# The last two blocks of a first MoE layer as one stage: its first product by seven block products on 512-column halves, with the second block's activations kept in DRAM

## The chip, the cores and the metric

The kernel runs on one core of a Trainium2 chip. The metric is the device time of one execution in microseconds. Every engine follows its own instruction list in order: TensorE (PE) multiplies, VectorE (DVE) and ScalarE (ACT) do the elementwise work, and SyncE (SP) issues nearly all DMAs. They wait for one another by semaphores.

## The reference

Chunked attention over 4 x 768 tokens (8 heads of 64) gives x of 3072 x 512. Two feed-forward layers follow:

```python
x = attention(q, k, v, mem_k, mem_v)          # 3072 x 512
h = x @ w_in                                  # first layer: 512 -> 2048
g = np.maximum(h, 0.0) + alpha * np.minimum(h, 0.0)
x = g @ w_out                                 # 2048 -> 512
h = x @ w2_in                                 # second layer
out = (h * np.tanh(softplus(h))) @ w2_out
```

## The kernel before

**Tiles.** The tokens are six blocks of 512 columns (`NBA`, `BN`); x of a block is held transposed, four tiles of 128 rows. The 2048 inner features are 16 tiles j (`NJ`). Each fp32 operand is held as two fp32r parts, high and low, and a product is three matmuls: high by high, high by low, low by high. A "split" is a ScalarE cast for the high part and a VectorE subtraction for the low part.

**First layer.** For each block and j, `gemm1` (L990) does 4 x 3 matmuls of 512 columns into a bank, `act1` (L1019) applies the two-sided ReLU (two ScalarE steps, one VectorE step at L1025) and splits the result (L1015, L1016), and `gemm2` (L1059) does 4 x 3 matmuls of 512 columns into the block's four accumulating banks, two tiles j later (`LAG`). `evac` (L1065) sends a finished block's sums to `yd` in DRAM.

**Weights.** The first layer's are loaded and split once, in block 0. w1_in stays in 16 slots `wi`. Of w1_out, j from 10 on (`AWAY`) are also stored to `w1o` in DRAM (L1377), and in later blocks `reload1` (L396) brings them back through three slots in turn, 512 KB each.

**Second layer's weights.** 16 jobs of `spill` (L343; `w2_jobs`) load, convert and combine the weights for a scheme of seven block products in place of eight, and store the results in DRAM. They are spread over blocks 1 to 4. In block 5 `reload_in` (L408) brings what stays resident back into the `wi` and `wo` slots, 20 reloads of 512 KB.

**Attention.** Tiles of 128 tokens, T, go in pairs: a burst of score matmuls ("s", L723), softmax on ScalarE and VectorE with 16 VectorE transposes (L877), a burst of value matmuls ("v", L789), and a split into the block's x. The steps of block b + 1 are woven into the 32 half-steps of block b (`weave`, two per j). There is one set of buffers for scores and transposes; the keys and values of an odd tile share the tiles `upper` (L522, L559).

**Second layer.** For each of six blocks and eight pairs of j, `pair2` (L1160) does the seven products of 6 matmuls with 256 columns and the activation, and `gemm2_pair` the second product, 42 matmuls, woven between by `take`. `load_x` (L1087) prepares its operands from `yd`.

**Order.** `Plan` (L68) fixes the order of every engine's list ahead of time. Each step has a duration by formula (`a_`, `d_`, `p_`, `dma_`), a due time derived from the TensorE steps that need it, and dependences. Whenever an engine is free, the ready step with the earliest due time is next. A TensorE step that is not ready is passed by another that is. The chip then runs these lists as they stand.

Of the kernel before, what the change touches and what calls it, by code (L numbers as in the profile page):

```python
# [173 lines left out]
def chunked_attention_moe_moe_kernel(  # L174
# [77 lines left out]
    def dma_(b):  # L252
        return max(0.45, b / 265e3)
# [30 lines left out]
    AWAY = 10  # L284
    w1o = dp.tile([P, NJ - AWAY, 1024], F32, name="w1o")
# [110 lines left out]
    def reload1(u):  # L396
        w = slot("o", AWAY + away[0] % 3, [P, 2, 512], F32R)
        away[0] += 1
        add(
            "sp", dma_(P * 4096), lambda: nc.sync.dma_start(w.t.rearrange("p z f -> p (z f)").bitcast(F32), w1o[:, u - AWAY, :]),  # L400
            [(w1o_buf, u)], [w],
        )
        weights[0, "o", u] = w

    in_places = sorted([(j, "i", j) for j in range(12)] + [(j + 2, "o", j) for j in range(8)])
    pieces = {}

    def reload_in(n):  # L408
        w = slot(*in_places[n][1:], [P, 1024], F32R)
# [366 lines left out]
    def values_late(T):  # L776
# [19 lines left out]
        def rest():  # L796
            blk = T * P // BN
            if blk not in xts:
                xts[blk] = new_x(BN)
            (x, views, _, _), = xts[blk]  # L800
            cols = slice(T * P - blk * BN, (T + 2) * P - blk * BN)

            def unit(z, e):
                return views()[z][:, :, cols].rearrange("p a (i e n) -> p i a e n", i=2, e=2)[:, :, :, e]

            def flat(e):
                return bks[e].t.rearrange("p (i a n) -> p i a n", i=2, a=NP)

            def high(e):
                nc.scalar.copy(unit(0, e), flat(e))  # L810

            def low(e):
                nc.vector.tensor_sub(unit(1, e), flat(e), unit(0, e).bitcast(F32))

            for e in range(2):
                add("act", a_(512), partial(high, e), [bks[e]], [(x, ("h", T), e)])
                add("dve", d_(512), partial(low, e), [bks[e], (x, ("h", T), e)], [(x, ("l", T), e)])
# [66 lines left out]

    def behind(T):
# [42 lines left out]
    for blk in range(1, NBA):  # L928
        steps = []
        for T in range(blk * TB, (blk + 1) * TB, 2):  # L930
            steps += [("s", T), None, ("t", T) if T < UPT else None, ("v", T)]
        block_steps.append(steps)
# [5 lines left out]
    def open_second():  # L938
# [6 lines left out]

        def late(shape, tag):
            def make():
                open_()
                return phase["bp"].tile(shape, F32, tag=tag, name=tag)

            return make

# [12 lines left out]
        second["late"] = late  # L965
# [549 lines left out]
```

## Time and profile before

| | us |
|---|---|
| median of 3 runs | 1083.0 (1082.01 to 1083.23) |
| the profiled execution | 1082.07 |
| its span | 1080.3 |
| TensorE busy | 1073.4 (99%) |
| VectorE busy | 728.1 (67%) |
| ScalarE busy | 656.3 (61%) |
| DMA, mean over the span | 233 GB/s |

The first layer lies between about 25 and 590 us, with attention woven in until about 485 us; the second layer takes the rest. Busy shares are means over stages with different limits, so the reading goes by windows. The duration of a step can run into the next one's start; what an engine can carry is read from the distance of starts.

### The profile page before, as it was taken

How to read it: one execution, taken by the hardware profiler on the slowest of the kernel's cores; microseconds unless marked ns; L12 is line 12 of the kernel's file. 1: busy time of each engine (PE TensorE's matmuls, PEld its weight loads, DVE VectorE, ACT ScalarE, POOL GpSimd, SP SyncE). 2: the span in 40 equal slices, each digit the busy share in tenths (PEclk: the TensorE clock that was granted, in tenths of full speed). 3: DMA queues.
4: the chain of work that ended last, by engine and by line, in shares of the span. 5: the costliest groups of instructions: out<-in, count | busy, mean ns of one | idle time of the engine just before them, and what ended most of it. 6: DMA issues, size and time to landing. Idle time of an engine off the chain costs nothing.

```text
span 1080.3 us, 24504 instructions
## 1 busy us (share of the span) xinstructions
PE 1073.4 (99%) x9305; PEld 967.0 (90%) x9305; DVE 728.1 (67%) x1609; ACT 656.3 (61%) x1674; POOL 6.5 (1%) x19
## 2 busy tenths in 40 slices
PE   9999999999999999999999999999999999999998
PEld 6888888888888888888888999999999999999998
DVE  6899487676869767685422855675675675675654
ACT  6888456466564646555433766666676676675664
POOL 2000000000000000000000000000000000000000
PEclk9999999999999999999999999999999999999999
DMA  9968755776476577547764777887887887887874
GB/s 284 312 208 243 243 184 177 238 254 196 170 255 214 173 240 255 193 142 230 256 192 146 253 231 256 270 259 255 271 261 252 274 259 254 270 260 235 267 247 159
DMA packets 139670, 252.11 MB, mean 233 GB/s; under 512 B 13856, under 2 KB 45088, under 8 KB 139552
## 3 DMA queue, kind: packets, MB, share of 16 engines
q1 hardware_dynamic: 139552, 250.54, 72.3%
q8 instruction: 73, 1.20, 0.5%
q14 instruction: 45, 0.37, 0.1%
HBM read 205.14 MB, written 45.35 MB: 232 GB/s over the span
## 4 chain that ended last, share of the span: by engine, by line
PE 99%; ACT 0%; DVE 0%; issue 0%; DVEq 0%; ACTq 0%
PE bank L1003 24%; PE bank L1051 24%; PE bank L1267 22%; PE bank L1184 22%; PE bank L789 2%; PE bank L723 1%; PE bank L1361 1%; PE bank L600 0%; PE bank L667 0%; PE bank L836 0%; PE bank L860 0%; ACT L1198 0%; DVE e L1292 0%; ACT rstrip L250 0%; DVE rstrip L1326 0%
## 5 line engine op out<-in xcount | busy, mean ns | idle before, releaser
L1003 PE MATMUL bank<-xh,wi 128*128 128x512 f32 (+1 forms) x784 | 254.9, 387 | 0.0
L1051 PE MATMUL bank<-gh,wo 128*128 128x512 f32 x768 | 253.7, 391 | 0.0
L1003 PEld LDWEIGHTS bank<-xh,wi 128*128 128x128 f32 x784 | 146.3, 188 | 30.1
L1192 ACT COPY v<-bank 128x512 f32<-128x512 f32 x192 | 102.5, 534 | 115.0 <-PE bank L1184 112.0
L1051 PEld LDWEIGHTS bank<-gh,wo 128*128 128x128 f32 x768 | 144.1, 188 | 30.3
L1003 PE MATMUL bank<-xl,wi 128*128 128x512 f32 (+1 forms) x392 | 151.0, 385 | 0.0
L1051 PE MATMUL bank<-gl,wo 128*128 128x512 f32 x384 | 149.5, 389 | 0.0
L1025 DVE SCALAR_TENSOR_TENSOR rstrip<-rstrip,nalpha 128x512 f32<-128x512 f32 x96 | 71.8, 748 | 71.2 <-ACT rstrip L1022 70.4
L1015 ACT CAST gh<-rstrip 128x512 fp32r<-128x512 f32 x96 | 60.2, 627 | 89.0 <-DVE rstrip L1025 48.7
L1021 ACT ACTIVATE rstrip<-bank 128x512 f32<-128x512 f32 x96 | 57.9, 603 | 87.6 <-PE bank L1003 85.5
L1195 DVE TENSOR_TENSOR v<-v,v 128x256 f32<-128x256 f32 x190 | 79.5, 423 | 43.2 <-ACT v L1192 41.6
L1016 DVE TENSOR_TENSOR gl<-rstrip,gh 128x512 fp32r<-128x512 f32 x96 | 66.3, 691 | 56.0 <-ACT gh L1015 55.4
L1198 ACT ACTIVATE v<-v 128x256 f32<-128x256 f32 x192 | 80.0, 418 | 35.9 <-DVE v L1195 33.4
L1195 DVE TENSOR_TENSOR v<-v 128x256 f32<-128x256 f32 x142 | 60.0, 422 | 51.9 <-ACT v L1192 48.5
L1003 PEld LDWEIGHTS bank<-xl,wi 128*128 128x128 f32 x392 | 73.6, 188 | 14.4
L1051 PEld LDWEIGHTS bank<-gl,wo 128*128 128x128 f32 x384 | 72.1, 188 | 14.6
L1184 PE MATMUL bank<-wo,wi 128*128 128x256 f32 x432 | 61.9, 283 | 0.6 <-ACT v L1192 0.6
L742 ACT ACTIVATE s<-bank,su 128x64 f32<-128x64 f32 x160 | 48.5, 346 | 19.7 <-DVE su L759 19.7
L1022 ACT ACTIVATE rstrip<-bank 128x512 f32<-128x512 f32 x96 | 57.4, 598 | 0.9 <-DMA yd<-rstrip 0.9
L877 DVE STREAM_TRANSPOSE aT<-s 32x256 f32<-32x256 f32 x128 | 55.8, 436 | 2.9
L1184 PEld LDWEIGHTS bank<-wo,wi 128*128 128x128 f32 x432 | 56.3, 192 | 1.1 <-ACT v L1192 1.0
L1184 PE MATMUL bank<-xl,wi 128*128 128x256 f32 x396 | 54.4, 283 | 0.0
(198 smaller groups left out, 1888.0 us busy)
## 6 DMA issues: line engine op xcount, KB each, us to landing
wi<-w2o SPq DMA_DIRECT2D x201, 256.0 KB, 3.6
wo<-w2o SPq DMA_DIRECT2D x132, 256.0 KB, 3.7
wo<-w1o SPq DMA_DIRECT2D x30, 512.0 KB, 4.5
w2o<-wo SPq DMA_DIRECT2D x57, 256.0 KB, 2.6
wi<-w2s SPq DMA_DIRECT2D x56, 256.0 KB, 3.5
wo<-in_w_out_dram SPq DMA_DIRECT2D x24, 512.0 KB, 7.8
w2k<-wo SPq DMA_DIRECT2D x40, 256.0 KB, 2.2
wo<-w2s SPq DMA_DIRECT2D x40, 256.0 KB, 3.4
```

Of the source, the lines that this page charges most:

```text
L1003: nc.tensor.matmul(bk.t[:, lo:hi], a, b, start=kk == 0 and i == 0, stop=kk == KT - 1 and i == 2)
L1015: add("act", a_(n), lambda: nc.scalar.copy(g.t[0], src.t[0]), [src], [(g, "h")])
L1016: add("dve", d_(n), lambda: nc.vector.tensor_sub(g.t[1], src.t[0], g.t[0].bitcast(F32)), [src, (g, "h")], [(g, "l")])
L1021: add("act", a_(n) - 0.05, lambda: nc.scalar.activation(m.t[0], h.t[:, :n], AF.Relu, scale=-1.0), [h], [m])
L1022: add("act", a_(n) - 0.05, lambda: nc.scalar.activation(r.t[0], h.t[:, :n], AF.Relu), [h], [r])
L1025: lambda: nc.vector.scalar_tensor_tensor(r.t[0], m.t[0], nalpha[:, j : j + 1], r.t[0], ALU.mult, ALU.add),
L1051: nc.tensor.matmul(bk.t[:, :n], lt, rh, start=j == 0 and i == 0, stop=j == NJ - 1 and i == 2)
L1184: nc.tensor.matmul(X.t[:, half * HB : (half + 1) * HB], l, r, start=start and kk == n == 0, stop=kk == 1 and n == 2, skip_group_check=True,)
L1192: add("act", c_(n * HB), lambda: nc.scalar.copy(e.t[:, : n * HB], X.t[:, : n * HB]), [X], [(e, i) for i in range(n)])
L1195: add("dve", e_(HB), lambda: op(at(to), at(a), at(b)), [v[a], v[b]], [v[to]])
L1198: add("act", c_(HB), lambda: nc.scalar.activation(at(name), at(name), AF.Mish), [], [v[name]])
L1267: nc.tensor.matmul(bk.t[:, s * HB : (s + 1) * HB], g.t[:, zg * HB + s * P : zg * HB + (s + 1) * P], piece()[:, zw * HB : (zw + 1) * HB], s ...
```

## The change

Blocks 0 to 3 (`WIDE` = 4) are done as before. Their x, and that of blocks 4 and 5, is prepared earlier: the attention steps of blocks 2 to 5 are set at fixed half-steps of blocks 1 to 3 (`AT`: per pair scores at 0, values at 10, the next scores at 11). x of block 4 goes to four free `wo` slots (`far_x`). Eleven of the 16 `spill` jobs run in the first 38 tiles after block 0, and five in the new stage. `AWAY` becomes 6, and all 16 tiles of w1_out are stored to `w1o`, so every later use of j from 6 on, and of all j in the new stage, is a reload.

The new stage takes blocks 4 and 5 together. `wide_x` forms four combinations of the four 256 x 512 quarters of x (12 VectorE steps and 4 casts of 1024 columns). For each pair p of j, `sums_of_w` forms the four combinations of the weights' quarters and splits them; `pair1` does seven products of 6 matmuls with 512 columns, recombines them in banks and on VectorE, applies the activation to four 128 x 512 results, splits the two of block 4 for its `gemm2` and stores the two of block 5 to `rb` in DRAM. The parts of block 4's `gemm2` of the pair before are woven between (`take(12)`, two parts of three matmuls). After the pairs, block 5's activations are loaded from `rb`, split and multiplied, 14 tiles j after one another, with the weights reloaded a second time. `reload_in` runs partly in the stage, partly behind it and, for the last four, behind the end of block 5. The second layer's accumulators change banks (`ACC`, `X` from bank 7 to 3), its v tiles become halves of five tiles of 1024 columns, and `dma_` assumes 315 GB/s after 120 us of TensorE work.

The diff, cut:

```diff
-        return max(0.45, b / 265e3)
+        return max(0.45, b / (265e3 if plan.now < 120 else 315e3))
-    AWAY = 10
-    w1o = dp.tile([P, NJ - AWAY, 1024], F32, name="w1o")
+    AWAY = 6
+    WIDE = NBA - 2
+    JOBS, JOB_STEPS = 11, 38
+    w1o = dp.tile([P, NJ, 1024], F32, name="w1o")
+    rb = dp.tile([P, NJ, BN], F32, name="rb")
-    in_places = sorted([(j, "i", j) for j in range(12)] + [(j + 2, "o", j) for j in range(8)])
+    in_places = [("i", j) for j in range(2, 12)] + [("o", j) for j in range(6)] + [("i", 0), ("i", 1), ("o", 6), ("o", 7)]
...
+    block_steps.append(sum(([("s", T), None, ("t", T), ("v", T)] for T in range(TB, UPT, 2)), []))
+    AT = sum(((11 * n, 11 * n + 10) for n in range(8)), ())
+    steps_at = {2 * NJ + p: ("sv"[n % 2], UPT + n // 2 * 2) for n, p in enumerate(AT)}
...
-        second["X"] = bank(7)
+        second["X"] = bank(3)
-    ACC = {1: 4, 0: 5, 3: 6, 5: 0, 4: 1, 6: 2, 2: 3}
+    ACC = {1: 0, 0: 1, 5: 2, 3: 6, 4: 7, 6: 4, 2: 5}
...
+    def wide_x():
...
+        t = dict(zip(("a21", "a22", "a11", "a12"), second["whole"]))
+        for name in ("a21", "a22", "a11", "a12"):
...
+                "dve", d_(1024), lambda to=t[name], f=f: nc.vector.tensor_add(to.t, f(0).bitcast(F32), f(1).bitcast(F32)),
...
+        for name, to, a, b, op in (
+            ("s1", "a22", "a21", "a22", nc.vector.tensor_add), ("s3", "a21", "a11", "a21", nc.vector.tensor_sub),
+            ("s2", "a11", "a22", "a11", nc.vector.tensor_sub), ("s4", "a12", "a12", "a11", nc.vector.tensor_sub),
+        ):
...
+            add("act", a_(1024), lambda f=f, o=t[to]: nc.scalar.copy(f(0), o.t), [t[to]], [(bufs[0], "h")])
+            add(
+                "dve", d_(1024), lambda f=f, o=t[to]: nc.vector.tensor_sub(f(1), o.t, f(0).bitcast(F32)),
...
+    def sums_of_w(p):
+        w = [weights[0, "i", 2 * p + n] for n in range(2)]
+        tt, to = second["tt"].next(), wide["t"].next()
+        for n in range(2):
...
+        for to_, x, y in ((3, 5, 3), (5, 4, 5), (4, 4, 3), (6, 6, 4)):
+            add("dve", d_(HB), lambda to_=to_, x=x, y=y: nc.vector.tensor_sub(q(to_), q(x), q(y)), [], [tt])
+        add("act", a_(1024), lambda: nc.scalar.copy(to.t[:, :1024], tt.t), [tt], [(to, "h")])
...
+    def pair1(p, xs, take):
+        to = tops.pop(p)
+        A, B_ = (bank(i + p % 2 * 2) for i in (4, 5))
+        e1, e2, e3, e4 = (second["v"].next() for _ in range(4))
...
+            add("pe", 6 * 0.227, go, [w] + bufs, [bk])
...
+        product(0, A, True)
+        product(3, B_, True)
+        keep(e1, A)
+        keep(e2, B_)
+        take(12)
+        product(4, A, False)
+        product(2, B_, False)
+        keep(e3, A)
+        more(e3, B_)
+        act(j1, e3)
+        split_wide(WIDE, j1, e3)
+        take(12)
+        product(5, A, False)
+        more(e2, A)
+        act(j1, e2)
+        if not last_:
+            away_(j1, e2)
+        take(12)
+        product(6, A, False)
+        product(1, B_, True)
+        more(e1, B_)
+        act(j0, e1)
+        split_wide(WIDE, j0, e1)
+        act(j0, e4, A)
+        if not last_:
+            away_(j0, e4)
+        return e4, e2
...
+    open_second()
+    xs = wide_x()
+    open_wide()
+    for layer, blk, j in pend:
+        reload1(j)
+        parts.extend((6, part) for part in gemm2_parts(layer, blk, j))
+    tops = {0: sums_of_w(0)}
+    for p in range(NPAIR):
+        if p + 1 < NPAIR:
+            tops[p + 1] = sums_of_w(p + 1)
+        if p < 6:
+            for job in [next(jobs, None) for _ in range(1)]:
+                if job:
+                    job(plan.now + 25.0)
+        ends_ = pair1(p, xs, take)
+        take(12)
+        if 0 < p < 6:
+            for n in (2 * p - 2, 2 * p - 1):
+                reload_in(n)
+        if p < NPAIR - 1:
+            for j in (2 * p + 1, 2 * p):
+                parts.extend(wide_parts(WIDE, j, (p, j) == (0, 1), False))
...
+    for n, (e, j) in enumerate(zip(ends_[::-1], (NJ - 1, NJ - 2))):
+        for name, part in wide_parts(WIDE, j, False, j == NJ - 2):
+            part()
+        split_wide(WIDE + 1, j, e)
+        for name, part in wide_parts(WIDE + 1, j, n == 0, False, True):
+            part()
+    open_rest()
+    xnext = load_x(0)
+    for n in range(10, 16):
+        reload_in(n)
+    order_b = list(range(NJ - 2))
+    for j in order_b:
+        e = second["v"].next()
+        add("sp", dma_(P * BN * 4), lambda e=e, j=j: nc.sync.dma_start(e.t, rb[:, j, :]), [(rb_buf, j)], [e])
+        split_wide(WIDE + 1, j, e)
+        parts.extend(wide_parts(WIDE + 1, j, False, j == order_b[-1]))
+        while len(parts) > 8:
+            take(6)
...
+    for n in range(16, len(in_places)):
+        reload_in(n)
+    open_rings()
```

## Rows read from the trace of the kernel before

**Rows 1.** page: the span, and each engine's busy time, share and instructions

```profile
span 1080.3 us, 24504 instructions
...
PE 1073.4 (99%) x9305; PEld 967.0 (90%) x9305; DVE 728.1 (67%) x1609; ACT 656.3 (61%) x1674; POOL 6.5 (1%) x19
```

**Rows 2.** page: the chain that ended last, shares of the span

```profile
PE 99%; ACT 0%; DVE 0%; issue 0%; DVEq 0%; ACTq 0%
```

**Rows 3.** waits of TensorE: line, releaser, us in total, times, longest us

```profile
PE bank L1361 <- DVE busy L1359: 1.2, 1, 1.2
...
PE bank L1184 <- ACT v L1192: 0.6, 1, 0.6
```

**Rows 4.** chain in order of time, 35 to 170 us: start us, us, what

```profile
42.42 2.72 PE bank L1051 x12
...
152.76 2.00 PE bank L789 x128
154.76 2.95 PE bank L1003 x12
...
165.87 1.44 PE bank L723 x94
```

**Rows 5.** windows: us, busy per engine, PEclk, DMA share, GB/s

```profile
40.00:60.00 20.00, 20.00 (x94) 16.59 (x93) 18.83 (x39) 18.63 (x59) 0.00 (x0) 1.00 0.98 258
320.00:340.00 20.00, 20.00 (x90) 16.57 (x89) 18.97 (x43) 10.02 (x27) 0.00 (x0) 1.00 0.86 292
520.00:540.00 20.00, 20.00 (x90) 16.57 (x89) 5.06 (x8) 6.84 (x12) 0.00 (x0) 1.00 0.68 223
515.00:520.00 5.00, 5.00 (x23) 4.13 (x22) 4.80 (x8) 2.84 (x5) 0.00 (x0) 1.00 0.98 365
100.00:105.00 5.00, 5.00 (x142) 4.21 (x141) 4.97 (x10) 3.79 (x7) 0.00 (x0) 1.00 0.26 99
```

**Rows 6.** timeline of VectorE, three stretches: start us, us, line, operation

```profile
44.81 0.75 DVE L1025 SCALAR_TENSOR_TENSOR rstrip<-rstrip,nalpha 128x512 f32<-128x512 f32 x1
45.48 0.68 DVE L338 TENSOR_TENSOR wi<-wf,wi 128x512 fp32r<-128x512 f32 x1
46.08 0.42 DVE L323 TENSOR_SCALAR wf<-wo 128x512 uint32<-128x512 uint32 x1
46.54 0.69 DVE L326 SCALAR_TENSOR_TENSOR wf<-wo,wf 128x512 uint32<-128x512 uint32 x1
...
148.21 1.81 DVE L877 STREAM_TRANSPOSE aT<-s 32x256 f32<-32x256 f32 x4
...
324.71 0.42 DVE L364 TENSOR_TENSOR wo<-wf,wf 128x256 f32<-128x256 f32 x1
325.05 0.42 DVE L364 TENSOR_TENSOR wo<-wf 128x256 f32<-128x256 f32 x1
...
325.72 0.68 DVE L750 TENSOR_TENSOR s<-s,su 128x512 f32<-128x512 f32 x1
326.33 0.42 DVE L364 TENSOR_TENSOR wo<-wf,wo 128x256 f32<-128x256 f32 x1
```

**Rows 7.** groups by form, VectorE: count, busy us, mean ns, idle before

```profile
L1025 DVE SCALAR_TENSOR_TENSOR rstrip<-rstrip,nalpha 128x512 f32<-128x512 f32 x96 | 71.8, 748 | 71.2 <-ACT rstrip L1022 70.4
L1016 DVE TENSOR_TENSOR gl<-rstrip,gh 128x512 fp32r<-128x512 f32 x96 | 66.3, 691 | 56.0 <-ACT gh L1015 55.4
...
L1292 DVE TENSOR_TENSOR rstrip<-bank,rstrip 128x512 f32<-128x512 f32 x24 | 16.5, 688 | 3.8 <-PE bank L1267 3.0
...
L364 DVE TENSOR_TENSOR wo<-wf,wo 128x256 f32<-128x256 f32 x32 | 13.5, 421 | 0.3
```

**Rows 8.** line L400, the reloads of w1_out: issue to landing

```profile
DMA to landing us min/median/max: 3.7/4.5/6.8
```

**Rows 9.** line L522, an odd tile's keys: queue timeline from 154 us, and landing

```profile
154.47 1.21 SPq L522 DMA_DIRECT2D qbd<-in_kw_dram  x2
...
DMA to landing us min/median/max: 2.3/2.9/7.9
```

More of the change, by code (lines that the diff above doesn't have):

```diff
@@ L948, in make, with open_rest @@
                 open_()
-                return phase["bp"].tile(shape, F32, tag=tag, name=tag)
-            return make
+                if tag not in boxes:
+                    boxes[tag] = phase["bp"].tile(shape, F32, tag=tag, name=tag)
+                return boxes[tag]
+            return make
+        second["late"] = late
+        wholes = [late([P, 1024], f"b{i}") for i in range(5)]
+        second["whole"] = [Buf(m, att_bufs) for m in wholes]
+        second["tt"] = Ring(wholes[4:])
+        second["tt"].last = [att_bufs]
+        second["v"] = Ring([lambda m=m, i=i: m()[:, i * BN : (i + 1) * BN] for m in wholes[:4] for i in range(2)])
+        second["v"].last = [[b] for b in second["whole"][:4] for _ in range(2)]
+    def open_rest():
+        late = second["late"]
         def places(*tags):
@@ new lines, in chunked_attention_moe_moe_kernel, with open_wide @@
+    wide = {}
+    def open_wide():
+        makes = [lambda z=z: xmakers[1][z]() for z in range(2)]
+        wide["t"] = Ring(makes)
+        wide["t"].last = [list(xring.last[1]) for _ in range(2)]
+        gm = [lambda i=i: [t[:, i * BN : (i + 1) * BN] for t in gstrip.tiles] for i in range(2)]
+        for j in range(2):
+            m = maker(cp, [P, 2, 512], F32R, f"wi{j}")
+            gm.append(lambda m=m: (lambda w: [w[:, z, :] for z in range(2)])(m()))
+        g4.makes = gm
+        g4.last = [[x[2] for x in gstrip.live]] * 2 + [slots["i", 0], slots["i", 1]]
@@ new lines, in split_wide, with wide_parts, part, go @@
+    def split_wide(blk, j, e):
+        g = g4.next()
+        add("act", a_(BN), lambda: nc.scalar.copy(g.t[0], e.t), [e], [(g, "h")])
+        add("dve", d_(BN), lambda: nc.vector.tensor_sub(g.t[1], e.t, g.t[0].bitcast(F32)), [e, (g, "h")], [(g, "l")])
+        gts[0, blk, j] = g
+    def wide_parts(blk, j, first, last_, again=False):
+        if not again:
+            reload1(j)
+        w = weights[0, "o", j]
+        g = gts.pop((0, blk, j))
+        if first:
+            accs[0, blk] = [bank(a) for a in ((0, 1, 2, 3) if blk == WIDE else (6, 7, 4, 5))]
+        def part(a):
+            bk = accs[0, blk][a]
+            def go():
+                cs = slice(a * P, (a + 1) * P)
+                (gh, gl), (wh, wl) = g.t, (w.t[:, z, :] for z in range(2))
+                for i, (lt, rh) in enumerate(((wh[:, cs], gh), (wh[:, cs], gl), (wl[:, cs], gh))):
+                    nc.tensor.matmul(bk.t, lt, rh, start=first and i == 0, stop=last_ and i == 2)
+            add("pe", 3 * p_(BN), go, [w, g], [bk])
+            if last_:
+                evac(0, blk, a, bk)
+        return [(6, partial(part, a)) for a in range(KT)]
@@ L1389, in chunked_attention_moe_moe_kernel @@
     LAG = 2
[L1390 removed]
+    tiles = [(0, blk, j) for blk in range(WIDE) for j in range(NJ)]
     pend = []
     xcur = xts[0]
[L1393 to L1394 removed]
+    jobs = iter(w2_jobs)
+    sent_ = [0]
     for half in range(2):
```

175 lines of the change are left out of this document (125 added, 50 removed).

## The prediction

> **What bounds the kernel now.** I read first the busy times and the chain that ended last: TensorE is busy 1073.4 of 1080.3 us, and the chain is TensorE for 99% of the span [rows 1, 2]. Then the waits of TensorE, which name only 1.2 us and 0.6 us [rows 3]: nothing that the other engines or the DMAs do delays it after the start. Then the chain in order of time: a stretch of twelve 512-column matmuls (one `gemm1` or one `gemm2`) takes 2.72 us, so 0.2267 us each [rows 4]. Last, VectorE by windows: 18.8 and 19.0 of 20 us beside a full TensorE in the first layer, but 5.1 of 20 in its last block [rows 5]. So time is bought only by TensorE instructions, as long as VectorE and the DMAs still keep ahead; the change takes instructions from the first and gives work to the other two.
>
> **What is removed.** For two blocks and a pair of j, `gemm1` issues 2 x 2 x 12 = 48 matmuls of 512 columns; seven products of six matmuls are 42. Over 8 pairs 6 x 8 = 48 matmuls go: 48 x 0.2267 = 10.88 us. `gemm2`, the second layer and attention keep their matmuls. All of it lies on the path. The profiled execution took 1082.07 us (span 1080.3 and 1.8 around it), so with no new wait it becomes 1071.2. The median of the runs shown, 1083.0, lies 0.9 above that execution; I forecast on the execution and let the range take the 0.9.
>
> **Attention, packed.** Blocks 2 to 5 keep their 8 steps of each kind, but a score burst now starts one 2.72 us stretch after the value burst before it, where before it came 165.87 - 154.76 = 11.1 us after [rows 4]. The odd tile's keys go into `upper`, which the value burst reads, so they can only be loaded after it. Both loads were issued in 1.2 us, beginning at the burst's end, and one lands 2.9 us after its issue [rows 9]: about 0.9 + 2.9 = 3.8 us against 2.72. The planner charges these DMAs too (two of 0.55, 2.0 to land and 0.2: 3.3 us) and moves other matmuls ahead of the burst; what is left is what it misjudges, 0 to 0.6 us for each of 7 bursts: 0 to 4 us. I take 1.2, nearer to zero, because an order made by the same cost model leaves TensorE 0.6 us of waits after the start [rows 3]. Queued behind a late key load on SP are the next values and the stores of `spill`; nobody needs those within 10 us.
>
> **VectorE in blocks 1 to 3.** Its cost is read from starts, not durations: a 256-column tensor_tensor starts 0.34 us after the one before (its row says 0.42), a 512-column one 0.61 (0.68), the scalar_tensor_tensor 0.67 (0.75), a dependent pair 0.46 [rows 6]. From 256 and 512 a 1024-column one is estimated at 0.61 + 2 x 0.27 = 1.15. A pair of attention tiles now comes every 5.5 tiles, 5.5 x 5.44 + 3.95 (its bursts and their restarts) = 33.9 us. VectorE work in it: attention 16 transposes of 0.46 and six 512-column steps with small ones, 11.3; `act1` and splits 5.5 x 1.4 = 7.7; 5.5 x 11/38 = 1.6 `spill` jobs of 5.8 (two loads' conversions 2.1, eleven 256-column steps 3.7): 9.3. Together 28.3 of 33.9, 84%. Blocks 0 and 3 ran at 94 and 95% over 20 us with TensorE full [rows 5]: cost 0, since a tile's `act1` has about 10 us until its `gemm2`. Were that cover gone, each us over would be a us of TensorE.
>
> **Storing all of w1_out.** Ten more 512 KB stores fall around block 0, where the DMAs are at a quarter from 100 to 105 us [rows 5] and no store has a reader before block 1: cost 0. If they pushed a weight load back instead, one store is 1.4 us of them at 365 GB/s [rows 5]; 0 to 1.4, in the range only.
>
> **Entry into the wide stage.** Block 5's x is complete after the value burst of T=22, eight stretches (21.8 us) before the stage; `keep(e1)` and product 4 need the splits of s1, s3 and s2 some 4.1 us later (products 0 and 3 and two parts). In those 25.8 us VectorE must do two x splits 1.2, four adds, three sums and three splits of 1024 columns 10 x 1.15 = 11.5, the weight sums of pair 0 (two of 512, four of 256, one of 1024 and restarts) 4.1, and five tiles 6.4: 23.2, or 90%. It fits, with 2.6 us to spare. 0 to 3 us; I take 0.8, for the rise to 100% in places.
>
> **The wide pairs.** A pair is 42 + 24 matmuls = 14.96 us of TensorE. VectorE: three adds from PSUM 1.8, four scalar_tensor_tensor 2.7, two splits 1.2, weight sums 4.1: 9.8 us; with a `spill` job in pairs 0 to 4 it is 15.6, with none 9.8. Over eight pairs that is 8 x 9.8 + 5 x 5.8 = 107 of 120 us. Five pairs are 0.6 us over, 3.2 in all, unless the jobs, due 25 us later than issued, slide into pairs 5 to 7. In each pair product 6 waits for the add from the same bank, with 1.36 us of parts as cover for a 0.61 us step. Bounds 0 and 3.2; I take 1.3. ScalarE gets fourteen steps and a job's nine in 15 us; from 40 to 60 us it did 59 in 20 beside a full TensorE [rows 5]: 0.
>
> **The block that comes back from DRAM.** Fourteen j follow each other every 2.72 us, not 5.44, with three slots for the weights. A slot lives landing + 2.72 us of use, and three stretches last 8.16, so a load has 5.44 us. It lands in 4.5 us (median) and 6.8 (worst) [rows 8]. At 4.5 nothing is lost; at 6.8 a round takes 9.52, (9.52 - 8.16)/3 = 0.45 us per j, 6.3 us in all. Demand in the 49 us after the pairs: 16 weights 8.4 MB, 14 activations 3.7, x of the second layer 1.0, six reloads 3.1: 16.2 MB, 331 GB/s, against 365 GB/s in the fullest 5 us near there [rows 5]; the six reloads can begin in pair 7, where only two weights and two stores move, 1.6 MB in 15 us. Bounds 0 and 6.3; I take 1.0.
>
> **Start of the second layer.** Its first product gets bank 3, free earlier than bank 7 was, and four reloads move behind it, needed six pairs later. The 0.6 us wait there [rows 3] may go or stay: -0.6 to 0; I take 0.
>
> Sum: 1071.2 + 1.2 + 0.8 + 1.3 + 1.0 = 1075.5 us.
>
> **Rivals.** A, VectorE becomes the bound of the wide stage, and the kernel gets slower. If an instruction held the engine for its whole row, a pair would cost 3 x 0.688 + 4 x 0.748 + 2 x 0.691 for the splits + 2 x 0.691 + 4 x 0.421 + an estimated 1.23 for the sums = 10.7, and a job 2 x (0.42 + 0.69) + 11 x 0.421 = 6.9 [rows 6, 7]: 17.6 against 14.96, 2.6 us in each of five pairs, 13.1. With the attention and return terms, 1071.2 + 13.1 + 2.2 = 1086.5. It decides from 10.88/5 = 2.2 us over per pair. Against it: the starts overlap the rows before them [rows 6]. For it: the hand-over add, product 6, add couples the two engines in every pair. [...]
>
> B, the return from DRAM cannot keep its weights ahead of their use: 6.3 us at the worst landing in place of 1.0, 1075.5 + 5.3 = 1080.8. For it: reloads, activations and x share one queue in order, and a reload ahead adds its transfer. Against: all but the steady two loads can be done early.
>
> C, attention comes late. In the trace the last transposes of a pair end at 150.0, and the value burst stands at 152.8 [rows 4, 6]; the new order has one stretch (2.72 us) less from scores to values, so no slack is left unless VectorE, which works by due time, does them earlier. Late by 2.7 us at the last pair, and with key loads at their bound of 4, it is 1071.2 + 4 + 2.7 + 0.8 + 1.3 + 1.0 = 1081.0.
>
> D, the saving is not there: the matmuls removed do not set the pace anywhere. TensorE's share of the chain speaks against it; 1082 to 1083.
>
> **How the numbers follow.** Forecast 0.66, 1071 to 1079; A 0.11; B 0.09; C 0.10; D 0.04. Of measurements of this kernel 0.2%, 2.2 us, can be told from no change: faster is below 1080.8, slower above 1085.2. The forecast and about 0.12 of B and C lie below: 0.78. Slower is A with a little of C beyond its price: 0.12. The rest is 0.10. The range begins at 1071.2 - 0.6 and some, 1070.6, takes in B and C with the 0.9 us of the median, and ends at 1082.5; it leaves out A, some of D and little below.
>
> **What would show it.** Right: 48 fewer TensorE matmuls; first stretches of blocks 1 to 3 still 2.72 us apart; TensorE waits of 3 to 6 us in all, spread over score bursts, the entry, and weights from `w1o`; VectorE 90 to 98% through the pairs. Wrong: a wait of TensorE on VectorE of 2 us or more in every one of pairs 0 to 4 (A); waits on `w1o` or on VectorE's splits of block 5 that recur each third j (B); score or value bursts that begin late (C); TensorE full and the span unchanged (D). The forecast fails most easily if the planner's costs for the new 1024-column steps, which no row of the trace shows, are too small.

## The result, and the profile after

The changed kernel takes 1096.1 us (median of 4 runs, 1092.05 to 1097.22) against 1083.1 for the kernel before on the same chip: a ratio of 1.0112, 95% interval 1.0083 to 1.0141. It is slower; forecast was 1075.5, faster, with a range up to 1082.5. The profiled execution took 1096.3 us, its span is 1094.6.

The page of the changed kernel: span, busy time with share and instructions, and the shares of the chain that ended last.

```profile
span 1094.6 us, 24604 instructions
...
PE 1072.4 (98%) x9252; PEld 963.0 (88%) x9257; DVE 776.3 (71%) x1698; ACT 682.1 (62%) x1721; POOL 6.5 (1%) x19
...
PE 75%; DVE 10%; DMA 8%; ACT 3%; issue 2%; SPq 1%; DVEq 0%; ACTq 0%
```

53 fewer matmuls are recorded than in [rows 1] (48 were removed, and the weight loads' records fall by 48, from 9305 to 9257; this trace lacks five matmul records more than that one), yet TensorE is as long busy as before, and a quarter of the chain, which was TensorE's for 99% [rows 2], now runs over VectorE, DMAs and ScalarE. To see where, one row of a line's view serves as a milestone: the first product of the wide stage (form, count, ns min/median/max, first and last start), here of the changed kernel and then of `g1_late40`, a version of it (below) in which TensorE never waits in blocks 1 to 3.

```profile
L1480 PE MATMUL bank<-wo,wi x96: 388/389/393, 427.9 to 546.7; 128*128 128x512 f32 x96
```

```profile
L1481 PE MATMUL bank<-wo,wi x96: 388/389/395, 410.7 to 530.8; 128*128 128x512 f32 x96
```

The first score burst of block 1 starts at 121.1 us before and after, and at 120.9 in `g1_late40`. Between it and the milestone both versions issue the same matmuls (3188 records in each trace), so 17.2 us go between 121 and 428 us. From there to the end the changed kernel takes 666.7 us and `g1_late40` 661.9: another 4.8. Waits of TensorE from 120 to 425 us, then from 600 us to the end (line, releaser, us in total, times, longest):

```profile
PE bank L793 <- DVE aT L881: 6.2, 5, 2.2
PE bank L1027 <- ACT rstrip L1046: 2.1, 2, 1.4
PE bank L1075 <- DVE rstrip L250: 1.1, 1, 1.1
...
PE bank L1210 <- ACT b L1218: 3.8, 5, 1.6
PE bank L1293 <- DMA wo<-w2o: 0.2, 1, 0.2
```

L793 is the value burst, L881 its transposes; L1027 and L1075 are `gemm1` and `gemm2`; L1046 is a step of the activation, L250 the copy of a finished block's sums, L1218 ScalarE's copy of a product of the second layer. The first three rows are 9.4 of the 17.2 us. The clock adds to it. Windows of the changed kernel (us, busy of PE, PEld, DVE, ACT, POOL, then the granted clock, DMA share, GB/s):

```profile
186.00:190.00 4.00, 2.45 (x118) 2.33 (x118) 3.19 (x7) 1.10 (x3) 0.00 (x0) 0.89 0.88 303
190.00:192.00 2.00, 2.00 (x7) 1.55 (x6) 2.00 (x4) 1.58 (x4) 0.00 (x0) 0.50 0.82 240
...
364.00:368.00 4.00, 1.26 (x27) 0.85 (x26) 3.77 (x10) 0.00 (x0) 0.00 (x0) 0.83 0.52 197
368.00:373.00 5.00, 5.00 (x119) 4.55 (x116) 3.20 (x6) 3.70 (x7) 0.00 (x0) 0.50 0.26 73
410.00:430.00 20.00, 20.00 (x90) 16.57 (x89) 20.00 (x25) 10.98 (x17) 0.00 (x0) 1.00 0.29 88
...
450.00:470.00 20.00, 20.00 (x90) 16.54 (x89) 19.29 (x41) 13.34 (x27) 0.00 (x0) 1.00 0.96 313
...
490.00:510.00 20.00, 20.00 (x90) 16.57 (x89) 19.92 (x42) 15.14 (x32) 0.00 (x0) 1.00 0.90 298
...
545.00:585.00 40.00, 39.67 (x174) 32.05 (x173) 18.26 (x28) 16.88 (x30) 0.00 (x0) 1.00 0.94 315
```

After the value bursts at 185.5 and 364.2 us, in which TensorE waited for transposes, the granted clock is 0.50, from 189.1 to 192.6 and from 366.6 to 373.5 us, most of it full work; the share of time missing to full clock, window by window, adds up to 5.1 us, a few tenths of it while TensorE stood still. In the kernel before, the clock never fell in this stretch (1.00 in all windows of 0.5 us). (In windows of 0.25 us it is 0.50 all through these two stretches, but for the windows at their ends, and 1.00 elsewhere from 120 to 428 us; what lies between in the rows above is a mean over a window.) The rest, 2.7 us, no row names; the restarts are in it, as the first 512-column matmul after a wait stands with 0.50 us in place of 0.39 (at 239.1 and 247.7 us). Of the lower four rows the first is the entry into the new stage, the next two are its pairs, with VectorE at 19.3 and 19.9 of 20 us and TensorE full beside it, and the last is the block that comes back from DRAM.

The transposes are late for a reason that the timeline shows. ScalarE (L324 converts raw weights, L374 is a cast of a `spill` job), VectorE (L327 to L377 are the job, L881 the transposes) and TensorE around the value burst at 185.5:

```profile
173.64 0.67 ACT L324 ACTIVATE raw<-raw 128x512 f32<-128x512 f32 x1 [1.82 <-DMA raw<-in_w_in_dram]
...
176.51 0.67 ACT L324 ACTIVATE wo<-wo 128x512 f32<-128x512 f32 x1 [1.70 <-DMA wo<-in_w_in_dram]
...
183.80 0.41 ACT L374 CAST wo<-wf 128x256 fp32r<-128x256 f32 x1 [1.51 <-DMA w2k<-wo]
...
177.21 0.43 DVE L327 TENSOR_SCALAR wf<-wo 128x512 uint32<-128x512 uint32 x1 [1.07 <-ACT wo L324]
177.68 0.43 DVE L881 STREAM_TRANSPOSE aT<-s 32x256 f32<-32x256 f32 x1
...
181.27 1.42 DVE L377 TENSOR_TENSOR wo<-wo 128x256 fp32r<-128x256 f32 x4
182.72 3.17 DVE L881 STREAM_TRANSPOSE aT<-s 32x256 f32<-32x256 f32 x7
...
187.31 0.44 DVE L881 STREAM_TRANSPOSE aT<-s 32x256 f32<-32x256 f32 x1
...
185.53 0.72 PE L793 MATMUL bank<-aT,vw 64*64 64x32 f32 x14
187.80 0.94 PE L793 MATMUL bank<-aT,vw 64*64 64x32 f32 x49 [1.55 <-DVE aT L881]
```

A job's raw load lands later than the order assumes: by its formula the reader can start 3.7 us after the issue, and the first of a job's two loads lands after 5.3 (w2_in) or 4.8 us (w2_out, both medians, rows below). ScalarE, whose list is fixed, stands still at its conversion; VectorE stands still at the next one; and the transposes, none of which has a wait of its own in these rows, come behind it in VectorE's list. The burst waits for the last of them. Of the eight value bursts four are late (a table below has them all). So it is at two of these, 185.5 and 328.9 us, where VectorE stands still for 1.4 us among the transposes. At the other two, 292.7 and 364.2, it works without a gap from the first transpose to the last, with 10 and 14 steps of a job between them; the job's waits lie ahead of that, such as 2.1 us of VectorE at 345.1, behind casts of ScalarE of which one had waited for a store (`w2o`).

### The profile page after: what moved, and what is told of

Its sections match the earlier page's. It is cut to its first block, busy times and chain, and to the rows that moved or that the text cites. A ratio compares the mean times of both kernels' runs of the same rounds, so it can differ in the third digit from the quotient of the medians.

```text
span 1094.6 us, 24604 instructions
## 1 busy us (share of the span) xinstructions
PE 1072.4 (98%) x9252; PEld 963.0 (88%) x9257; DVE 776.3 (71%) x1698; ACT 682.1 (62%) x1721; POOL 6.5 (1%) x19
## 4 chain that ended last, share of the span: by engine, by line
PE 75%; DVE 10%; DMA 8%; ACT 3%; issue 2%; SPq 1%; DVEq 0%; ACTq 0%
PE bank L1210 20%; PE bank L1293 20%; PE bank L1027 10%; PE bank L1075 10%; PE bank L1556 6%; PE bank L1480 5%; DVE aT L881 3%; PE bank L793 2%; DVE wo L377 1%; DMA wo<-in_w_in_dram 1%; ACT s L746 1%; DMA wo<-w1o 1%; DMA raw<-in_w_in_dram 1%; DVE wo L368 1%; PE bank L727 1%
## 5 line engine op out<-in xcount | busy, mean ns | idle before, releaser
L1027 PE MATMUL bank<-xh,wi 128*128 128x512 f32 (+1 forms) x528 | 173.7, 390 | 2.1 <-ACT rstrip L1046 2.1
L1218 ACT COPY b<-bank 128x512 f32<-128x512 f32 x192 | 102.4, 533 | 115.4 <-PE bank L1210 112.7
L1075 PE MATMUL bank<-gh,wo 128*128 128x512 f32 x512 | 170.3, 392 | 1.1 <-DVE rstrip L250 1.1
L1027 PEld LDWEIGHTS bank<-xh,wi 128*128 128x128 f32 x528 | 99.0, 189 | 23.0 <-ACT rstrip L1046 2.8
L1075 PEld LDWEIGHTS bank<-gh,wo 128*128 128x128 f32 x512 | 96.5, 189 | 22.0 <-DVE rstrip L250 1.5
L1221 DVE TENSOR_TENSOR b<-b,b 128x256 f32<-128x256 f32 x190 | 79.7, 422 | 48.2 <-ACT b L1218 46.7
L1221 DVE TENSOR_TENSOR b<-b 128x256 f32<-128x256 f32 x142 | 59.9, 422 | 62.0 <-ACT b L1218 58.6
L1027 PE MATMUL bank<-xl,wi 128*128 128x512 f32 (+1 forms) x264 | 101.9, 386 | 0.0
L1224 ACT ACTIVATE b<-b 128x256 f32<-128x256 f32 x192 | 79.6, 418 | 35.3 <-DVE b L1221 32.4
L1075 PE MATMUL bank<-gl,wo 128*128 128x512 f32 x256 | 100.0, 391 | 0.0
L1045 ACT ACTIVATE rstrip<-bank 128x512 f32<-128x512 f32 x64 | 38.8, 608 | 44.0 <-PE bank L1027 42.1
L1049 DVE SCALAR_TENSOR_TENSOR rstrip<-rstrip,nalpha 128x512 f32<-128x512 f32 x64 | 47.8, 747 | 22.4 <-ACT rstrip L1046 21.9
L1027 PEld LDWEIGHTS bank<-xl,wi 128*128 128x128 f32 x264 | 50.1, 190 | 9.3
L881 DVE STREAM_TRANSPOSE aT<-s 32x256 f32<-32x256 f32 x128 | 55.8, 436 | 2.8
L1075 PEld LDWEIGHTS bank<-gl,wo 128*128 128x128 f32 x256 | 48.2, 188 | 10.2 <-DVE gl L1040 0.4
```

The lines of the kernel that those rows point to most:

```text
L881: nc.vector.transpose(dst[:, :, m // 2, m % 2], src[:, :, keys])
L1027: nc.tensor.matmul(bk.t[:, lo:hi], a, b, start=kk == 0 and i == 0, stop=kk == KT - 1 and i == 2)
L1049: lambda: nc.vector.scalar_tensor_tensor(r.t[0], m.t[0], nalpha[:, j : j + 1], r.t[0], ALU.mult, ALU.add),
L1075: nc.tensor.matmul(bk.t[:, :n], lt, rh, start=j == 0 and i == 0, stop=j == NJ - 1 and i == 2)
L1218: add("act", c_(n * HB), lambda: nc.scalar.copy(e.t[:, : n * HB], X.t[:, : n * HB]), [X], [(e, i) for i in range(n)])
L1221: add("dve", e_(HB), lambda: op(at(to), at(a), at(b)), [v[a], v[b]], [v[to]])
```

## Experiments

Theories: P, the planner's new price makes it expect transfers too early; Q, the attention packed beside eleven jobs leaves the value bursts no slack. Once Q was the likelier, it was divided: H, steps that wait for a late transfer stand at the head of an engine's list and hold up what is behind them; K, the engines have too much work there; X, the jobs' transfers slow the attention's loads.

`g1_late40` and the three runs beside it (`g2`, `g3`, `g4`) are compared with the kernel before at 1083.1 us, all others with 1082.2 to 1082.6. `e3_jobs_all_late`, `e5b_work` and `e9_transfers` are one execution each and have no interval; a milestone or a wait is always that of one execution, the profiled one.

**The planner's price of a transfer.** The change prices DMAs after 120 us at 315 GB/s, where it was 265. `e1_dma265` puts 265 back; `e2_before315` gives 315 to the kernel before.

```diff
-        return max(0.45, b / (265e3 if plan.now < 120 else 315e3))
+        return max(0.45, b / 265e3)
```

> The changed kernel with one edit: the order is planned with 265 GB/s for DMAs throughout, as before the change, not with 315 after 120 us. Theory P (price): the order counts on loads that land later on the chip, so steps that wait for them stand at the head of ScalarE's and VectorE's lists; then most of the 17 us lost in blocks 1 to 3 and the 4 us of waits in the second layer go, and the time is 1072 to 1080. Theory Q (packing): the 8 attention pairs with 11 spill jobs beside them leave the value bursts no slack whatever the price; then the 17 us stay and only the 4 us of the second layer go, 1089 to 1094.

> The kernel before with one edit: DMAs planned with 315 GB/s after 120 us of TensorE work. Theory P: waits of TensorE on ScalarE's copies behind late loads of yd appear in the second layer (3 to 5 us) and some in blocks 1 to 4, 1086 to 1095. Theory Q: at the old spacing nothing but the second layer's 3 to 5 us can appear, 1083 to 1088, with no wait of a value burst on transposes.

`e1_dma265` took 1097.8 us (1.0146, 1.0118 to 1.0174): first wide product at 426.6, waits of 9.8 us in blocks 1 to 3 (7.4 of them on ScalarE's activations, L1046) and 4.3 in the second layer. So the price is not the cause, in either place, and theory P falls; Q's range, 1089 to 1094, was missed as well. `e2_before315` took 1087.7 (1.0059, 1.0042 to 1.0076): the price has a cost of its own there, in waits on the copies of a finished block's sums (2.0 us) and on ScalarE's copies of the second layer's products (1.7), but none on transposes.

**Are the jobs the cause?** `e3_jobs_all_late` moves all 16 `spill` jobs to the wide stage; `e4_jobs8` leaves eight in blocks 1 to 3.

```diff
-    JOBS, JOB_STEPS = 11, 38
+    JOBS, JOB_STEPS = 0, 38
...
-            for job in [next(jobs, None) for _ in range(1)]:
+            for job in [next(jobs, None) for _ in range(3)]:
```

```diff
-    JOBS, JOB_STEPS = 11, 38
+    JOBS, JOB_STEPS = 8, 38
...
-        if p < 6:
+        if p < 8:
             for job in [next(jobs, None) for _ in range(1)]:
```

> The changed kernel with all 16 spill jobs issued in the wide stage (three a pair) and none in blocks 1 to 3, so that the packed attention is alone there. Read from blocks 1 to 3 alone: if the jobs beside the attention cause the late value bursts (Q as a load on VectorE, or P by their loads), no value burst waits and the first wide product starts at 411 to 413 us in place of 427.9. If the spacing of 10 half-steps is too short by itself, the waits stay and it starts at 420 or later. The wide stage then has 16 x 5.8 + 78 = 171 us of VectorE work against 120, so the whole time says nothing about a good version: 1110 to 1140.

> The changed kernel with 8 spill jobs in blocks 1 to 3 (same 38 tiles) and 8 in the wide stage, one a pair. Q as a load on VectorE: 3 x 5.8 us less there, waits of the value bursts fall by half or more, first wide product at 412 to 420; the wide stage with 8 jobs is 78 + 46 = 124 of 120 us on VectorE but has its return stage behind it, 0 to 5 us more there; 1082 to 1092. P: the loads' price is unchanged and so are the waits, 1094 to 1097.

Without jobs the wide stage begins at 412.1 us, with 1.5 us of waits, all on key and value loads; with eight at 418.6, with waits on transposes of 3.2. So the jobs beside the packed attention cost the time, not the packing by itself. In the wide stage they cost more: 1163 us in all with 16 there, above the 1110 to 1140 expected, in waits of `pair1` on ScalarE of up to 17 us. `e4_jobs8` took 1095.2 us (1.0133, 1.0099 to 1.0166), above the 1082 to 1092 expected: what it wins in blocks 1 to 3 it gives back later; its profiled execution, one of 1102.6 us, has a wait of 8.3 us on a weight from `w1o` in the return stage.

**Their work, or their transfers at the head of a list?** `e5b_work` loads raw weights for the first job alone; all later jobs convert the same two buffers. `e9_transfers` keeps loads and stores and leaves the work out, in blocks 1 to 3 and in the wide stage.

```diff
+        if layer and raw2.n >= 2:
+            kept.append(kept[-2])
+            return kept[-1]
```

```diff
-            fs.append(to_f32(item, load_raw(item, at=at), at=at))
+            fs.append(load_raw(item, at=at))
...
-            z = st[i]
-            add("act", a_(HB), lambda z=z, src=src: nc.scalar.copy(z.t[:, :HB], src()), [read], [(z, "h")], at=at)
+            z = weights[0, "i", 13]
```

> The two raw buffers of the second layer's weights are loaded once each, by the first job; every later half-step converts the same two buffers again, so that all the VectorE and ScalarE work of the jobs and all their stores stay, while none of their work waits for a load (the second layer then works with wrong weights). Theory H (steps that wait for a late load stand at the head of VectorE's and ScalarE's lists in order, and hold up the value bursts' transposes behind them): TensorE's waits between 120 and 425 us fall from 9.4 to 3 us or less, and the first wide product starts at 417 us or sooner (427.9 in the changed kernel, 411 if only the attention's placing counted). Theory K (the work itself crowds the engines there): 7 us of waits or more stay, the first wide product at 423 or later.

> The jobs keep only their transfers: the raw loads, which nothing reads, and stores of the same size, from a first-layer weight that lies ready; their VectorE and ScalarE work is left out (the second layer then works with wrong weights). H and K alike: waits between 120 and 425 us at 2.5 us or less and the first wide product at 411 to 414 us. Theory X (the jobs' transfers slow the attention's own loads): 4 us of waits or more, the first wide product at 417 or later. The second layer's waits of some 4 us stay under all three, as nothing there changes.

`e9_transfers`: 1075.8 us. Its milestone, and its waits of TensorE in blocks 1 to 3:

```profile
L1472 PE MATMUL bank<-wo,wi x96: 388/389/389, 412.5 to 529.2; 128*128 128x512 f32 x96
```

```profile
PE bank L719 <- DMA qbd<-in_kw_dram: 1.0, 2, 0.8
```

So the transfers as such disturb next to nothing (theory X falls). The time is close to the forecast's 1075.5, but this does not bear out the terms of the sum one by one: the jobs' work is gone from the wide stage too, whose price it was part of. The second layer's waits fell to 1.5 us, against my expectation that they would stay. `e5b_work`: 1084.0 us, first wide product at 417.1. The window from 120 to 412 us of the changed kernel and then of this run, and this run's waits of TensorE in blocks 1 to 3:

```profile
120.00:412.00 292.00, 282.61 (x3124) 231.83 (x3123) 226.90 (x495) 162.94 (x517) 0.00 (x0) 0.98 0.73 238
```

```profile
120.00:412.00 292.00, 287.93 (x3171) 236.63 (x3170) 252.98 (x555) 179.08 (x554) 0.00 (x0) 1.00 0.69 225
```

```profile
PE bank L733 <- DVE xl L823: 2.0, 4, 1.1
PE bank L733 <- DMA qbd<-in_kw_dram: 1.9, 2, 1.4
```

With more VectorE work than in the changed kernel (253.0 us in this stretch against 226.9), no value burst waits for a transpose any more. The waits fall to 3.9 us and 10.8 of the 17.2 us are gone: nearer to H than to K, though both of H's bounds (3 us, 417 us) are just missed, and a good third is left. There the jobs' steps still wait for their own stores to land, 17.4 us on ScalarE and 7.2 on VectorE. The run does not take the waits away and leave the rest in place: its order is planned anew, and from the second burst on no step of a job lies among the transposes any more, where the changed kernel has 10 to 15 at five of these seven bursts. So it does not tell the wait for a load from the place of the steps.

**Planning later landings.** `e6_lag3` counts 3.0 us instead of 2.0 from a transfer's end to its reader; `e7_lag3raw` adds 2.5 for raw loads.

```diff
         if a == "sp":
-            return 2.0
+            return 3.0
```

```diff
+        if layer:
+            plan.slow[i] = 2.5
```

> The changed kernel, with one number of the plan changed: 3.0 us where it had 2.0 from the end of a transfer on SP's queue to its first reader. H: the raw loads land 3 us later than planned, so a third of that is met in blocks 1 to 3: first wide product at 419 to 427 us; the second layer's waits on yd's loads (landing 4 to 5.9 us) fall from some 4 to 2 us or less; 1089 to 1094 us in all. K: first wide product at 425 to 429, and the second layer as under H: 1091 to 1096.

> As the one with 3.0 us, and the plan also counts 2.5 us more for each raw load of the second layer's weights, so that their readers are put behind work that is ready. H: waits between 120 and 425 us at 4 us or less, the first wide product at 413 to 420 us, the second layer's waits at 2 us or less: 1080 to 1088 us. K: the first wide product at 424 us or later, 1090 us or more.

`e6_lag3` took 1088.1 us (1.0058, 1.0041 to 1.0075), just under the 1089 to 1094 expected: first wide product at 423.8, and in the second layer one wait of 0.7 us, on another load; the 3.8 us on L1218 are gone, though the `yd` loads land no sooner (3.8 to 4.9 us). So those waits came from `yd` loads later than planned: in the stretch from 600 to 800 us they land in 4.5 to 5.1 us (medians by target) in the changed kernel and mostly in 3.5 to 3.9 before. `e7_lag3raw` missed: 1091.9 us (1.0094, 1.0066 to 1.0121), first wide product at 427.4. Its waits on transposes fell to 2.0, but 6.1 us came on activations (L1049 there, L1046 in the changed kernel). That a later reader is only moved in front of something else that is due would fit this, but is not shown.

**Where the jobs stand among the bursts.** Three handles: jobs spread over 44 tiles j in place of 38 (the expectations say half-steps, but the edit counts tiles, 48 in blocks 1 to 3), jobs 20 us later, later landings. The 20 us move a job's loads too (`not_before` takes the same number), so this is a shift of the job, not only a lower rank for its steps as the expectations put it. `g1_late40` plans 4.0 us from block 1 on alone.

```diff
-    JOBS, JOB_STEPS = 11, 38
+    JOBS, JOB_STEPS = 11, 44
...
-                next(jobs)(plan.now)
+                next(jobs)(plan.now + 20)
...
         if a == "sp":
-            return 2.0
+            return 2.0 if i < self.late else 4.0
```

> The changed kernel with one number changed: the eleven jobs over 44 half-steps instead of 38, due when they are issued, landing 2.0. If room was short (K): the first wide product at 418 us or sooner and 1088 us or less. If the order in the lists was (H): 422 us or later, 1091 us or more.

> The changed kernel with one number changed: the jobs' steps due 20 us later, over 38 half-steps as in the change, landing 2.0. If the order was short (H): the first wide product at 419 us or sooner and 1089 us or less. If room was (K): 422 us or later, 1091 us or more.

> The changed kernel; the eleven jobs of blocks 1 to 3 are spread over 44 of the 48 half-steps (38 before) and their steps are due 20 us later, so that the plan puts a value burst's transposes ahead of them whenever both are ready. The landing of loads is planned as before (2.0 us). H, with the order of the lists as its handle: first wide product at 414 to 421 us (427.9 in the changed kernel, 412.5 with the jobs' work left out), the second layer's waits of some 4 us unchanged: 1082 to 1090 us. K (the work itself crowds the engines): first wide product at 422 or later, 1091 us or more.

> The same due times and spread, and 3.5 us planned from the end of a transfer on SP's queue to its first reader (2.0 in the changed kernel). H: waits between 120 and 425 us at 2.5 us or less, first wide product at 412 to 416 us, second layer's waits at 1 us or less: 1074 to 1080 us, faster than the kernel before. K: first wide product at 420 or later, 1086 us or more.

> As the one with 3.5 us, with 4.0. H: as that one within 2 us, 1074 to 1081 us; if landing still decides at 3.5, this one is the faster of the two. K: 1086 us or more.

> The version with jobs due 20 us later over 44 half-steps, with 4.0 us of landing planned for the transfers from block 1 on alone, 2.0 ahead of it. If the 2.8 us that the version with 4.0 throughout loses ahead of the first score burst (123.9 us against 121.1) come from the plan of block 0 alone: first score burst at 121.1, first wide product at 412 to 414 us, 1075 to 1078 us in all. If planned landing late in the prologue also helped later stages: 1079 us or more.

| kernel | spread, shift, landing | us (median) | ratio to before, 95% | first wide product |
|---|---|---|---|---|
| changed kernel | 38, 0, 2.0 | 1096.1 | 1.0112 (1.0083 to 1.0141) | 427.9 |
| `g4_spread_only` | 44, 0, 2.0 | 1097.4 | 1.0134 (1.0117 to 1.0151) | 422.4 |
| `g3_due_only` | 38, 20, 2.0 | 1095.8 | 1.0125 (1.0109 to 1.0141) | 429.9 |
| `f3_due20` | 44, 20, 2.0 | 1086.9 | 1.0038 (1.0022 to 1.0055) | 415.7 |
| `f1_plan35` | 44, 20, 3.5 | 1083.0 | 1.0000 (0.9991 to 1.0010) | 422.6 |
| `f2_plan40` | 44, 20, 4.0 | 1079.4 | 0.9965 (0.9952 to 0.9979) | 415.8 |
| `g1_late40` | 44, 20, 4.0 from block 1 | 1074.1 | 0.9921 (0.9907 to 0.9934) | 410.7 |

Neither spread nor shift does it alone, and together they win 9.2 us of the median, which points to the jobs' phase against the bursts. By the words of their expectations `g4_spread_only` fell on H's side and `g3_due_only` on K's (422 us or later, 1091 us or more), so as a pair they decide nothing between the two. The milestones in the last column are less sure than the medians: the executions of `f3_due20` lie between 1081.6 and 1090.9 us and the profiled one is 3.2 below their median, that of `g4_spread_only` is 3.0 below, that of `g3_due_only` 3.2 above. 3.5 missed its forecast of 1074 to 1080 and of 412 to 416 us for the first wide product; its profiled execution, with some 3 us of waits more in blocks 1 to 3 than the 1079.4 us version, is 4 us above its median, and why 3.5 and 4.0 differ by as much is open. With 4.0 throughout, the first score burst comes at 123.9 us instead of 121.1, because block 0 is planned later too; with 4.0 from block 1 on it is back at 120.9. `g1_late40` beats both kernels and is a little faster than expected (412 to 414 us, 1075 to 1078 in all). Its page, its window over blocks 1 to 3, TensorE's waits for other engines in the whole execution (none in blocks 1 to 3), and ScalarE's waits for the transfers of jobs from 120 to 412 us:

```profile
span 1072.6 us, 24598 instructions
...
PE 1063.8 (99%) x9252; PEld 957.9 (89%) x9257; DVE 776.0 (72%) x1698; ACT 682.2 (64%) x1721; POOL 6.5 (1%) x19
```

```profile
120.00:412.00 292.00, 292.00 (x3199) 241.08 (x3198) 235.02 (x505) 170.78 (x529) 0.00 (x0) 1.00 0.76 241
```

```profile
PE bank L1211 <- ACT b L1219: 1.6, 3, 0.7
PE bank L1575 <- DVE busy L1573: 1.2, 1, 1.2
PE bank L1575 <- DVE wi L251: 0.8, 1, 0.8
PE bank L1481 <- DVE b L1491: 0.4, 1, 0.4
```

```profile
ACT wo L375 <- DMA w2k<-wo: 3.2, 1, 3.2
ACT wo L325 <- DMA wo<-in_w_out_dram: 0.5, 1, 0.5
ACT raw L325 <- DMA raw<-in_w_in_dram: 0.4, 1, 0.4
```

The same waits of ScalarE in the changed kernel:

```profile
ACT raw L324 <- DMA raw<-in_w_in_dram: 8.1, 5, 3.4
ACT wo L374 <- DMA w2k<-wo: 7.8, 7, 2.8
...
ACT wo L324 <- DMA wo<-in_w_in_dram: 5.9, 5, 1.7
...
ACT raw L324 <- DMA raw<-in_w_out_dram: 3.9, 1, 3.9
```

With three smaller groups more (the second buffer's loads of w2_out, stores of `w2o` and `w2s`) they come to 30.5 us there, to 17.9 in `f3_due20`, to 4.1 in `g1_late40`, and to 7.8 in the kernel before. The loads themselves land no sooner. Median us from issue to landing (line, queue, count, KB), first of the changed kernel, then of `g1_late40`:

```profile
raw<-in_w_in_dram SPq DMA_DIRECT2D x6, 512.0 KB, 5.3
...
wo<-in_w_in_dram SPq DMA_DIRECT2D x6, 512.0 KB, 6.9
...
raw<-in_w_out_dram SPq DMA_DIRECT2D x5, 512.0 KB, 4.8
wo<-in_w_out_dram SPq DMA_DIRECT2D x5, 512.0 KB, 5.5
```

```profile
raw<-in_w_in_dram SPq DMA_DIRECT2D x6, 512.0 KB, 5.9
wo<-in_w_in_dram SPq DMA_DIRECT2D x6, 512.0 KB, 6.6
...
raw<-in_w_out_dram SPq DMA_DIRECT2D x5, 512.0 KB, 5.7
wo<-in_w_out_dram SPq DMA_DIRECT2D x5, 512.0 KB, 7.2
```

What differs is where the job's steps stand. From the timelines of VectorE and TensorE, for each of the eight value bursts from 120 to 412 us (six before): how many VectorE steps of a job lie between its first and its last transpose, and by how much the last transpose ends ahead of the burst's start (negative: after it).

| burst | 1 | 2 | 3 | 4 | 5 | 6 | 7 | 8 |
|---|---|---|---|---|---|---|---|---|
| changed: job steps | 11 | 14 | 0 | 14 | 10 | 15 | 14 | 0 |
| ahead, us | 2.1 | -2.2 | 0.3 | -0.2 | -1.7 | -1.3 | -3.5 | 6.4 |
| before: job steps | 14 | 15 | 3 | 15 | 3 | 15 | | |
| ahead, us | 2.7 | 4.2 | 2.4 | 4.4 | 3.2 | 4.2 | | |
| `g1_late40`: job steps | 0 | 10 | 3 | 0 | 12 | 3 | 0 | 12 |
| ahead, us | 10.1 | -0.2 | -0.1 | 0.7 | 0.0 | 0.6 | 2.5 | 0.1 |

Before, a job stood among the transposes as often, but value bursts came 44.7 or 50.2 us apart, and the transposes ended 2.4 to 4.4 us ahead. In the changed kernel the bursts come some 35 us apart; six have a job among their transposes, and with four of these the last transpose ends 1.3 to 3.5 us late (where it is 0.2 late, no wait stands at the burst). In `g1_late40` most of a job, 10 to 12 of its 15 steps, falls there three times, and then its loads have mostly landed when their conversions come up: VectorE has no gap among these transposes, and the last one ends at most 0.2 us after the burst's start.

**The same for the kernel before.** `f4_before_lag35` plans 3.5 us throughout, `g2_before_late40` has the shift of 20 us and 4.0 from block 1 on (its jobs are spread over all of their half-steps already).

> The kernel before, with 3.5 us planned from the end of a transfer to its first reader. Its own waits of TensorE come to some 2 us in all, so a better landing in the plan has little to win: 1080 to 1083 us. If it gains 4 us or more, what the plan with 3.5 us wins in the changed kernel is not a cure of the change's own loss but something that both kernels had open.

> The kernel before with the same two handles: jobs' steps due 20 us later and 4.0 us of landing planned from block 1 on (its jobs are spread over all of its half-steps already). It has 2.4 us of waits to win after the prologue: 1079 to 1083 us. If it reaches 1077 or less, the handles and not the change give the versions their lead.

Both came out above what was expected. The first took 1088.0 us (1.0047, 1.0033 to 1.0061): its first score burst comes at 125.5 us. The second took 1083.9 (1.0009, 1.0000 to 1.0018). So the handles give the kernel before nothing; the lead of `g1_late40`, 9.7 us over `g2_before_late40`, comes from the change.

## Why the prediction was wrong

**What is removed** fits the runs. `g1_late40` has all of the change, and TensorE is busy for 9.6 us less than before. Its span is 1072.6 us against 1080.3, 7.7 less (9.0 by the medians). With 10.9 removed, 3.2 are taken back (1.9 by the medians), where the sum put 4.3. That this is close is in part luck: of the waits that the sum priced, `g1_late40` has none at the score bursts and on `w1o`, and 0.4 us in the wide stage.

**VectorE in blocks 1 to 3, cost 0**: this step failed. The stage lost 17.2 us against `g1_late40`. Its load was about right (84% of a pair forecast; 226.9 of 292 us measured, 78%), but the inference was not. I took a busy share under the 94 and 95% that had been seen beside a full TensorE [rows 5] to mean that there is room. `g1_late40` does more VectorE work in the same 292 us, 235.0, and TensorE never waits, so the amount does not decide (theory K falls). What does is the order: which steps of a job stand ahead of the transposes, and whether they, or ScalarE's casts before them, wait for a transfer. The kernel before had late loads too, but its transposes ended 2.7 us ahead of the burst that I looked at [rows 4, 6]. The prediction named that margin under rival C; in the sum nothing was charged for spending it. The cover on which the 0 rested, some 10 us from a tile's `act1` to its `gemm2`, is not the transposes' cover.

**Attention, packed, 1.2 us.** The key loads that I priced cost little: no wait on them in the changed kernel and in `g1_late40`, 1.0 us in `e9_transfers`, 1.1 in `e3_jobs_all_late`, 1.9 in `e5b_work`. **Rival C** had the right symptom, value bursts behind their transposes, at the wrong price: it put 2.7 us at the last pair. It came at four bursts, 6.2 us of waits, with 3.2 more at activations and at a copy of a block's sums, 5.1 at half clock, which no term of the sum had, and 2.7 that no row names. That the same lists held up the 3.2 is likely, but not shown.

**Entry, wide pairs, 0.8 and 1.3 us; rival A.** From the first wide product to 600 us the changed kernel waits 0.2 us for VectorE and `g1_late40` 0.4. VectorE is at 19 to 20 of 20 us in the rows of the pairs above with TensorE full, so rival A, with 13.1 us of waits in five pairs, is refuted. In the pairs, as in [rows 6], steps of VectorE start before the end of the one ahead of them (at 448.19 us after one of 0.68 us from 447.59 on).

**The return from DRAM, 1.0 us; rival B.** One wait of 0.2 us on `w1o`; TensorE busy 39.67 of 40 us at 315 GB/s. The cost stays within its price, and rival B falls, with the jobs placed as in the change. With three more jobs in the wide stage (`e4_jobs8`) one wait of 8.3 us was seen, so the cover is thin.

**Start of the second layer, 0**: true of its start in the changed kernel, but I looked no further. From the wide stage on it takes 4.8 us more than `g1_late40`. It has 3.8 us in five waits between 650 and 1000 us, behind conversions of `yd` that were planned to land sooner, and 4.4 us of waits in all from there on, where `g1_late40` has 2.0; the rest of the 4.8 no row names. `e6_lag3` shows the cause of the 3.8, and the other versions of the changed kernel agree: with 3.0 us or more planned in this layer, they have 0.5 us or less of such waits from 600 us on; with 2.0 they have 2.1 or more. Only `e9_transfers`, with 2.0 planned and 0.6 us of waits, is not explained by it. Why `yd` lands later than before, when the layer moves the same data, is open; taking the planner's old price back does not remove the waits (4.3 us in the second layer of `e1_dma265`).

**What stays open.** How the 17.2 us divide between the phase of the jobs and the landing of their loads: the handles do not add up (5.5 us by the spread alone, -2.0 by the shift alone, 12.2 by both, each from one execution; by the medians of the whole -1.3, 0.3 and 9.2). A run that changes the rank of the job's steps and nothing else was not made.

## What to carry to other kernels

A busy share did not tell here whether an order that was fixed ahead of time would keep (226.9 of 292 us on VectorE came with 9.4 us of waits of TensorE, 235.0 with none): where a change packs latency-bound work closer, look in the trace for steps of other work that wait for a DMA in the same engine's list, and compare their real landing with the planned one. Ask then what stands behind them and how much of its lead the change takes. A change that loses by this is not refuted by its first time; here the same instructions, with the filler work placed between the bursts, went from 1.1% slower to 0.8% faster.

## What was not expected of the hardware

Waits of 1.6 and 2.7 us inside a value burst were each followed by TensorE at 0.50 of its clock in the rows above: 5.1 us missing to full clock in blocks 1 to 3, more than half as much as the 9.4 us of waits themselves. Two shorter waits of the changed kernel cost no clock: 1.3 us inside the burst at 292.7 and 1.4 us before the matmul at 247.7, with 1.00 granted from 220 to 300 us. What decides it is not shown. A 512 KB load of w2_in took 6.9 us (median) to land in its second buffer, beside 4.6 for a 512 KB reload from `w1o` in the same stretch. Its columns are cut from wide rows, but that is not shown to be the reason: the second of a job's two loads lands later than the first for w2_out as well, and in `g1_late40` w2_out's takes 7.2 us and w2_in's 6.6.
